# Scores in half strips, a narrower merge, and new orders in a fused attention and expert kernel

## The chip, the cores and the metric

The kernel runs on one core of a Trainium2 chip. The metric is the device time of one execution in microseconds; the median of three runs stands for a kernel. The engines are PE (TensorE: matmuls and transposes; PEld is its weight load), DVE (VectorE), ACT (ScalarE), POOL (GpSimd) and SP, which only issues transfers. Each works through a queue of its own in order.

## What is computed

Windowed causal attention with a linear bias per head, then a layer of experts in which every token goes to one expert (batch 8, 8 heads, 576 positions of 64; 4608 tokens of 512, 8 experts of 1024):

```python
scores = scale * np.matmul(q, k.transpose(0, 1, 3, 2))
bias = slopes[:, None, None] * (-np.abs(rel))[None, :, :]
mask = (rel >= 0) & (rel < 128)              # rel = query position - key position
attn = softmax(np.where(mask, scores + bias, -1e9))
x = (attn @ v) as rows of 512
expert_idx = argmax(normalized x @ normalized expert_emb.T / tau)
out = gate * (relu(x @ w1[e]) @ w2[e])       # e: the row's expert
```

## The kernel before

Attention goes over 36 tiles of 128 queries: per batch four whole ones (the first of them is of kind `first`, the others `full`), and for each two batches one of kind `pair`, whose halves are the last 64 queries of each batch. A tile has two halves of four heads, so there are 72 units `u`. A unit's steps, each a job with an engine:

- `score` (PE, `score_pe`, L544): queries times keys into two PSUM banks (`j` = 0, 1), one for each row half of PE. A `full` tile takes, for each of two head pairs `l`, 128 queries by 256 keys (this tile's and the one before); a `pair` tile takes 64 queries by 192 keys for each of the two batches.
- `merge` (DVE, `merge_dve`, L558 and L561): a window of 128 keys ends up in 128 columns, key position modulo 128. Columns whose key lies after the query are overwritten with those 128 keys earlier, under an integer mask. A `full` tile merges 128 columns of two heads in one instruction, a `pair` tile 64.
- `max` (DVE, L568) adds the bias table and takes the maximum; `exp` (ACT, L577); `flip` (PE, L585) transposes four strips of 128 by 128; `phi` (ACT, L488) and `plo` (DVE, L491) split the result into two f16 parts; `mask` (POOL, L617 to L635) separates this tile's keys from the earlier ones.
- `av` (PE, `values_pe`): a first matmul with `erow` (3 rows, L652) puts a small constant into the column of sums, then the weights are multiplied with v's two parts (L667), whose last column holds ones. `recip` and `norm` (DVE, L691, L697) divide.
- For every tile: `v_one` (POOL, L499) writes v's ones column, `v_hi` (ACT, or DVE for a share of the late tiles, L505 and L507) and `v_lo` (POOL, L513) split v; `xhi` (ACT, L710), `xlo` (POOL, L723), `xnorm` (ACT, L719), `xdma` (SP, L727) and `logit` (PE, L735) prepare the routing.

Tiles are routed in groups of 8, 8, 8, 6, 4 and 2; `put` (POOL, L833 and L834) writes a tiny memset to `spare` and then scatters a tile's rows to the experts' areas in DRAM. After the third group the expert with most rows so far is known; its weights are fetched and split (`wlo`: DVE, L877, 16 of them), and PE multiplies its first 384 rows between the last units (`head_hidden` L906, `head_output` L930). Then the experts follow, one after the other (L1329, L1373), which the change leaves alone.

The order is written out before anything runs. `Plan.run` takes the jobs with their planned durations, and on each engine, among the jobs that could start within `SLACK` of the earliest, picks the one with the smallest due time. A due time is `STEP * u + 1000 * DUE[stage]`. The jobs' instructions are then emitted in that order, and each engine's queue keeps it. `SHARE` says which share of the tiles has a step on the other engine, from tile `LATE` on under the names that end in 2.

The bias tables and the mask come from `bias_rel` (POOL) and `bias_table` (DVE): for `full` at the start, for `pair` as jobs `rel_pair` and `tab_pair` a little later; `first_table` is the `full` one with everything ahead of the tile's own keys struck out (POOL, L288).

Of the kernel before, what the change touches and what calls it, by code (L numbers as in the profile page):

```python
# [13 lines left out]
F16 = mybir.dt.float16  # L14
# [39 lines left out]
STEP = 2397  # L54
SLACK = {'PE': 105, 'ACT': 108, 'DVE': 21, 'POOL': 541, 'SP': 10}
# [5 lines left out]
DUE = {'load': -7.6, 'loadv': -4.4, 'k': -19.8, 'q': -19.8, 'v': 3.3, 'score': -16.9, 'merge': 1.9, 'max': 2.6, 'exp': 0.3, 'flip': 15.7, 'phi': -8.7, 'plo': 6.8, 'mask': 6.8, 'av': -22.6, 'norm': 10.7, 'xhi': 9.3, 'xlo': 16.5, 'xnorm': 21.0, 'xdma': 10.9, 'logit': -15.3, 'route': -3.1, 'put': 20.0, 'place': 18.0, 'gap': 4.3}  # L61
# [8 lines left out]
SHARE = {'v': 0, 'x': 0, 'v2': 0.33, 'x2': 0, 'p': 0, 'p2': 0.33}  # L70


class Plan:
# [19 lines left out]
    def run(self, free):  # L93
# [58 lines left out]
        self.order = order  # L152
        for _, n in order:
            jobs[n]["emit"]()
        return free, end
# [3 lines left out]
def kernel(  # L159
# [69 lines left out]
    nc.gpsimd.memset(erow, eparts[2])  # L229
    for n in (1, 0):  # L230
# [36 lines left out]
    def bias_rel(kind):  # L267
        rels[kind] = rel = const.tile([P, P], F32, tag="rel", name=f"rel_{kind}")
        for r0, r1 in ((0, P),) if kind == "full" else ((0, REM), (REM, P)):
            nc.gpsimd.iota(  # L270
                rel[r0:r1, :], pattern=[[-1, P]], base=0, channel_multiplier=1, allow_small_or_imprecise_dtypes=True
            )

    def bias_table(kind):
        rel = rels[kind]
        m = const.tile([P, P], I32, name=f"mask_{kind}")
        wrap = const.tile([P, P], F32, tag="wrap", name=f"wrap_{kind}")
        nc.vector.tensor_scalar(m, rel, 0.0, None, op0=ALU.is_ge)
        nc.vector.tensor_scalar(wrap, rel, 0.0, float(WIN), op0=ALU.is_lt, op1=ALU.mult)
        nc.vector.tensor_tensor(wrap, wrap, rel, op=ALU.add)  # L280
        tab = const.tile([P, H, P], BF16, name=f"tab_{kind}")
        for h in range(H):
            nc.vector.tensor_scalar(tab[:, h, :], wrap, -slopes[h] / QS, None, op0=ALU.mult)
        mk[kind], tabs[kind] = m, tab

    def first_table():
        tab = const.tile([P, H, P], BF16, name="tab_first")
        nc.gpsimd.affine_select(  # L288
            tab, tabs["full"], pattern=[[0, H], [-1, P]], compare_op=ALU.is_ge, fill=NEG, base=0, channel_multiplier=1
        )  # L290
        tabs["first"] = tab
# [86 lines left out]
    def attention(actx):  # L378
# [61 lines left out]
        bias_rel("full")  # L440
        bias_table("full")
# [43 lines left out]
        vS = {}  # L485

# [6 lines left out]
        def v_tag(T):  # L493
            return "vl" if tiles[T][2] == NF - 1 else "v"

        def v_one(T):
            tg = v_tag(T)
            hi = vp.tile([P, H, D + 1], F16, tag=tg + "h", name=f"vh_{T}", bufs=VBUFS[tg])
            nc.gpsimd.memset(hi[:, :, D : D + 1], 1.0 / SX)  # L499
            vS[T] = [hi, None]  # L500

        def v_hi(T):
            dst = vS[T][0][:, :, 0:D]
# [23 lines left out]
        def score_pe(T, hf):  # L527
            kind, b, t = tiles[T]
            R = P // REM
            if kind == "pair":  # L530
                spans = [
                    (slice(i * REM, (i + 1) * REM), slice(0, P + REM), b + i, slice(R * (t - 1), R * t + 1)) for i in range(2)
                ]
            else:
                a = t if kind == "first" else t - 1
                spans = [(slice(0, P), slice(0, (t + 1 - a) * P), b, slice(R * a, R * (t + 1)))]
            for j in range(2):
                sc[T, hf, j] = bank("sc", [P, 2, 2 * P], name=f"sc{j}_{T}_{hf}")
            for l in range(2):
                hp = 2 * hf + l  # L540
                for o, w, x, kc in spans:
                    for j in range(2):
                        rows = slice(64 * j, 64 * j + 64)
                        nc.tensor.matmul(  # L544
                            sc[T, hf, j][o, l, w].rearrange("p (n c) -> p n c", c=REM),
                            qT[T][rows, hp, o],
                            kT[x][rows, kc, hp, :],
                            start=True,
                            stop=True,
                            skip_group_check=True,  # L550
                        )

        def merge_dve(T, hf, j):
            kind, b, t = tiles[T]
            ps = sc[T, hf, j]
            if kind == "full":
                m = mk["full"].unsqueeze(1).to_broadcast([P, 2, P])
                nc.vector.copy_predicated(ps[:, :, 0:P], m, ps[:, :, P : 2 * P])  # L558
            elif kind == "pair":
                m = mk["pair"][:, 0:REM].unsqueeze(1).to_broadcast([P, 2, REM])  # L560
                nc.vector.copy_predicated(ps[:, :, 0:REM], m, ps[:, :, P : P + REM])  # L561

        def max_dve(T, hf, j, l):
            if (T, hf) not in nm_t:
                nm_t[T, hf] = sm.tile([P, 2, 2], F32, tag="nm", name=f"nm_{T}_{hf}", bufs=4)
            if (T, hf) not in sb_t:
                sb_t[T, hf] = pp.tile([P, 2, 2, P], F32, tag="sb", name=f"sb_{T}_{hf}", bufs=SBUFS)
            nc.vector.tensor_tensor_reduce(  # L568
                sb_t[T, hf][:, j, l, :], sc[T, hf, j][:, l, 0:P], tabs[tiles[T][0]][:, 4 * hf + 2 * l + j, :], -QS, BIG, ALU.add, ALU.min, nm_t[T, hf][:, j, l : l + 1]
            )  # L570

        def exp_act(T, hf, j):
            ps, nm = sb_t[T, hf][:, j], nm_t[T, hf][:, j, :]
            if (T, hf) not in pr_t:
                pr_t[T, hf] = pp.tile([P, 4, P], F32, tag="pe", name=f"pe_{T}_{hf}", bufs=3)
            for l in range(2):
                nc.scalar.activation(  # L577
                    pr_t[T, hf][:, 2 * l + j, :], ps[:, l, 0:P], AF.Exp, bias=nm[:, l : l + 1], scale=-1.0
                )

        def probs_pe(T, hf):
            pe = pr_t.pop((T, hf))
            pt = bank("ptp", [P, 4, P], name=f"ptp_{T}_{hf}")
            for i in range(4):
# [157 lines left out]
        def route_ops(gi):  # L742
# [232 lines left out]
        J("rel_pair", "POOL", 600, lambda: bias_rel("pair"), due=STEP * 4, early=EXPERT)  # L975
        J("tab_pair", "DVE", 1500, lambda: bias_table("pair"), after=["rel_pair"], due=STEP * 6)
# [6 lines left out]
        for T in range(NT):  # L983
# [3 lines left out]
            if T >= 2:  # L987
# [8 lines left out]
            J(f"v_one{T}", "POOL", 45, lambda T=T: v_one(T), makes=[(vt + "h", ("vh", T))], due=due("v", u0) - 1000)  # L996
            dv = share(T, SHARE["v" if T < LATE else "v2"])
            J(
                f"v_hi{T}", "DVE" if dv else "ACT", 335 if dv else 520, lambda T=T: v_hi(T),
                after=[f"load_v{T}", f"v_one{T}"], uses=[("ldv", T), ("vh", T)], due=due("v", u0),  # L1000
# [5 lines left out]
            for hf in range(2):  # L1006
# [3 lines left out]
                dep = [f"load_q{T}"] + [f"load_k{x}" for x in k_tiles(T)] + (["tab_pair"] if pair else [])  # L1010
# [7 lines left out]
                for j in range(2):  # L1018
                    c, key, n = a + (j,), keys[j], f"{u}_{j}"
                    J(  # L1020
                        f"merge{n}", "DVE", 0 if first else 202 if pair else 335, lambda c=c: merge_dve(*c),
# [24 lines left out]
                if rest:  # L1046
# [11 lines left out]
                    f"av{u}", "PE", 540 if first else 1130 if pair else 870, lambda a=a: values_pe(*a),  # L1058
# [55 lines left out]
        for gi, G in enumerate(groups):  # L1114
# [44 lines left out]
        for i in range(NP):  # L1159
# [4 lines left out]
            J(f"wlo{i}", "DVE", 850, lambda i=i: part_lo(i), after=[f"whi{i}"], uses=[("stg", i)], due=d + 5500, fill=True)  # L1164
# [476 lines left out]
```

## Time and profile before

| | us |
|---|---|
| median of 3 runs (lowest, highest) | 640.35 (640.18, 642.5) |
| the profiled execution, its own time | 641.88 |
| its span, first to last instruction | 640.2 |
| busy: PE, DVE, ACT, POOL | 595.4, 365.3, 323.0, 256.1 |
| mean granted clock of PE | 0.969 of 2.4 GHz |

The page divides the span into 40 slices of 16 us and shows each engine's busy share in tenths. Attention takes up the first seventeen. Matmuls are pipelined, so a group of matmuls that overlap counts once as busy, and what PE takes for a step is better read from the starts: from one step's first start to the next step's.

### The profile page before, as it was taken

How to read it: one execution, taken by the hardware profiler on the slowest of the kernel's cores; microseconds unless marked ns; L12 is line 12 of the kernel's file. 1: busy time of each engine (PE TensorE's matmuls, PEld its weight loads, DVE VectorE, ACT ScalarE, POOL GpSimd, SP SyncE). 2: the span in 40 equal slices, each digit the busy share in tenths (PEclk: the TensorE clock that was granted, in tenths of full speed). 3: DMA queues.
4: the chain of work that ended last, by engine and by line, in shares of the span. 5: the costliest groups of instructions: out<-in, count | busy, mean ns of one | idle time of the engine just before them, and what ended most of it. 6: DMA issues, size and time to landing. Idle time of an engine off the chain costs nothing. (4 is left out here: it accounts for less than half of the span.)

```text
span 640.2 us, 15149 instructions
## 1 busy us (share of the span) xinstructions
PE 595.4 (93%) x5633; PEld 387.8 (61%) x5633; DVE 365.3 (57%) x1320; ACT 323.0 (50%) x741; POOL 256.1 (40%) x454
## 2 busy tenths in 40 slices
PE   7799999899888879899899999999999999999993
PEld 3677777677665556365554764764856845744442
DVE  5989999889898787323465243451543383310250
ACT  5799899989897754032543242431432362201200
POOL 5769799989896585401102100202102022011011
PEclk9999999989997879999999999999999999999997
DMA  8688977989999643699999449339369091001000
GB/s 253 153 240 188 244 190 213 226 234 205 242 228 253 135 147 67 191 228 261 276 316 254 193 69 288 123 68 282 131 152 324 2 287 51 1 33 46 1 34 33
DMA packets 121291, 109.79 MB, mean 172 GB/s; under 512 B 85109, under 2 KB 86133, under 8 KB 121216
## 3 DMA queue, kind: packets, MB, share of 16 engines
q1 hardware_dynamic: 115376, 89.89, 55.7%
q0 software_dynamic: 5840, 18.92, 8.0%
q8 instruction: 45, 0.74, 0.5%
q14 instruction: 30, 0.25, 0.1%
HBM read 61.92 MB, written 28.12 MB: 141 GB/s over the span
## 5 line engine op out<-in xcount | busy, mean ns | idle before, releaser
L1329 PE MATMUL ps<-xT,w1h 128*128 128x272 f16 (+7 forms) x896 | 174.8, 295 | 3.9 <-DVE hl L1337 2.3
L1329 PE MATMUL ps<-xT,w1l 128*128 128x272 f16 (+7 forms) x448 | 132.3, 295 | 0.0
L371 POOL DMA_INDIRECT out_dram<-y,ids x32 | 34.5, 1078 | 204.6 <-DVE y L1387 103.8
L1329 PEld LDWEIGHTS <-w1h 128*128 128x128 f16 x896 | 87.9, 98 | 35.1 <-issue 2.5
L1337 DVE SCALAR_TENSOR_TENSOR hl<-ps,hh 128x272 f16<-128x272 f32 (+7 forms) x112 | 51.7, 475 | 96.0 <-ACT hh L1339 96.0
L577 ACT ACTIVATE pe<-sb,nm 128x128 f32<-128x128 f32 x288 | 94.5, 391 | 13.5 <-DVE nm L568 12.8
L1373 PE MATMUL ps<-w2h,hl 128*128 128x512 f16 (+1 forms) x264 | 98.5, 373 | 0.8 <-DVE hl L1337 0.7
L1373 PE MATMUL ps<-w2h,hh 128*128 128x512 f16 (+1 forms) x264 | 98.5, 373 | 0.1
L1373 PE MATMUL ps<-w2l,hh 128*128 128x512 f16 (+1 forms) x264 | 98.5, 373 | 0.0
L1339 ACT ACTIVATE hh<-ps 128x272 f16<-128x272 f32 (+7 forms) x112 | 45.7, 424 | 103.9 <-PE ps L1329 103.9
L1373 PEld LDWEIGHTS <-hh 128*128 128x128 f16 x528 | 51.4, 98 | 58.7 <-issue 0.8
L544 PE MATMUL sc<-k,q 64*128 64x256 f32 (+2 forms) x640 | 76.0, 379 | 0.0
L488 ACT ACTIVATE pq<-ptp 128x512 f16<-128x512 f32 x78 | 57.1, 736 | 11.9 <-PE ptp L585 9.5
L585 PE MATMUL ptp<-ident,pe 128*128 128x128 f32 x288 | 52.6, 297 | 5.5 <-ACT pe L577 5.0
L1304 DVE SCALAR_TENSOR_TENSOR w1l<-ws,w1h 128x1024 f16<-128x1024 f32 x28 | 33.4, 1222 | 40.1 <-ACT w1h L1306 40.0
L544 PEld LDWEIGHTS sc<-k,q 64*128 64x128 f32 (+1 forms) x640 | 47.6, 182 | 13.2 <-issue 6.1
L667 PE MATMUL av<-vh,mp 128*128 128x65 f16 x512 | 50.6, 198 | 4.4 <-POOL mp L617 1.7
L1304 DVE SCALAR_TENSOR_TENSOR w2l<-ws,w2h 128x1024 f16<-128x1024 f32 x28 | 33.8, 1223 | 34.3 <-ACT w2h L1306 33.9
L1329 PEld LDWEIGHTS <-w1l 128*128 128x128 f16 x448 | 44.0, 98 | 15.2 <-DVE w1l L1304 0.4
L1306 ACT ACTIVATE w1h<-ws 128x1024 f16<-128x1024 f32 x28 | 28.4, 1052 | 47.2 <-DMA ws<-moe_w_dram 47.1
L491 DVE SCALAR_TENSOR_TENSOR pq<-ptp,pq 128x512 f16<-128x512 f32 x66 | 48.8, 742 | 5.7 <-ACT pq L488 5.6
L1306 ACT ACTIVATE w2h<-ws 128x1024 f16<-128x1024 f32 x28 | 29.1, 1054 | 39.6 <-DMA ws<-moe_w_dram 37.5
(214 smaller groups left out, 1084.9 us busy)
## 6 DMA issues: line engine op xcount, KB each, us to landing
ws<-moe_w_dram SPq DMA_DIRECT2D x56, 512.0 KB, 10.5
q<-q_dram SPq DMA_DIRECT2D x36, 256.0 KB, 3.3
ldv<-v_dram SPq DMA_DIRECT2D x36, 256.0 KB, 4.0
k<-k_dram SPq DMA_DIRECT2D x32, 256.0 KB, 4.0
stg<-moe_w_dram SPq DMA_DIRECT2D x16, 256.0 KB, 4.4
xs<-zrow SPq DMA_DIRECT2D x3, 1092.2 KB
xs<-zrow SPq DMA_DIRECT2D x1, 1413.5 KB
xs<-zrow SPq DMA_DIRECT2D x1, 1285.0 KB
```

What stands on the lines that cost most here:

```text
L488: nc.scalar.activation(hi, ps, AF.Copy, scale=scale)
L491: nc.vector.scalar_tensor_tensor(lo, ps, scale, hi, op0=ALU.mult, op1=ALU.subtract)
L544: nc.tensor.matmul(sc[T, hf, j][o, l, w].rearrange("p (n c) -> p n c", c=REM), qT[T][rows, hp, o], kT[x][rows, kc, hp, :], start=True, sto ...
L577: nc.scalar.activation(pr_t[T, hf][:, 2 * l + j, :], ps[:, l, 0:P], AF.Exp, bias=nm[:, l : l + 1], scale=-1.0)
L585: nc.tensor.matmul(pt[:, i, :], pe[:, i, :], ident, start=(i == 0), stop=(i == 3), is_transpose=True, skip_group_check=True)
L667: nc.tensor.matmul(o_, a_, b_, start=False, stop=(n == last), skip_group_check=True)
L1304: nc.vector.scalar_tensor_tensor(lo_, x, SW, hi, op0=ALU.mult, op1=ALU.subtract)
L1306: nc.scalar.activation(hi, x, AF.Copy, scale=SW)
L1329: nc.tensor.matmul(ps[:, :w], a[:, kt, fs], xx[:, b + kt, c0 : c0 + w], start=(n == 0), stop=(n == len(jobs) - 1))
L1337: nc.vector.scalar_tensor_tensor(hl[:, ft, c0 : c0 + w], ps[:, :w], 0.0, hi, op0=ALU.max, op1=ALU.subtract)
L1339: nc.scalar.activation(hi, ps[:, :w], AF.Relu)
L1373: nc.tensor.matmul(ps, x[:, ft, a * P : (a + 1) * P], w[:, ft, c], start=(n == 0), stop=(n == len(jobs) - 1))
```

## The change

- Scores: every tile now works in half strips. For each half `i` of the queries, 64 queries by 192 keys of two heads `l`, which lie one above the other in the partitions; four matmuls (row half `j`, `l`) for each `i`. Strips are numbered 2j + i, and `flip` puts them back into the order of heads.
- Merge: in a `full` tile only 64 columns of each half can hold later keys; both halves are merged in one instruction of 2 x 64 columns.
- The tables get a further dimension, a slope column per partition in place of a constant, and serve all three kinds: the `pair` table and its jobs go.
- v's buffers are two tiles with slots; their ones are written once, ahead of the loop, and `v_one` goes.
- `erow` and `eone` get 128 rows, of which 125 are zero.
- `put` leaves the memset to `spare` out unless the job before it on POOL was a `put` too.
- Planned durations, `STEP`, `SLACK`, `DUE` and `SHARE` are new, and with them the order.

```diff
-STEP = 2397
-SLACK = {'PE': 105, 'ACT': 108, 'DVE': 21, 'POOL': 541, 'SP': 10}
+STEP = 2500
+SLACK = {'PE': 151, 'ACT': 51, 'DVE': 18, 'POOL': 693, 'SP': 147}
-DUE = {'load': -7.6, 'loadv': -4.4, 'k': -19.8, 'q': -19.8, 'v': 3.3, 'score': -16.9, 'merge': 1.9, 'max': 2.6, 'exp': 0.3, 'flip': 15.7, 'phi': -8.7, 'plo': 6.8, 'mask': 6.8, 'av': -22.6, 'norm': 10.7, 'xhi': 9.3, 'xlo': 16.5, 'xnorm': 21.0, 'xdma': 10.9, 'logit': -15.3, 'route': -3.1, 'put': 20.0, 'place': 18.0, 'gap': 4.3}
+DUE = {'load': -4.9, 'loadv': -2.2, 'k': -19.1, 'q': -15.7, 'v': 3.8, 'score': -28.6, 'merge': 2.1, 'max': 2.7, 'exp': -3.4, 'flip': 3.7, 'phi': -5.2, 'plo': 6.2, 'mask': 7.6, 'av': -18.6, 'norm': 10.9, 'xhi': 10.1, 'xlo': 17.0, 'xnorm': 24.5, 'xdma': 5.7, 'logit': -15.3, 'route': -0.6, 'put': 18.7, 'place': 17.6, 'gap': 6.4}
-SHARE = {'v': 0, 'x': 0, 'v2': 0.33, 'x2': 0, 'p': 0, 'p2': 0.33}
+SHARE = {'v': 0, 'x': 0, 'v2': 0, 'x2': 0.33, 'p': 0, 'p2': 0.33}
...
-    erow = const.tile([3, P], BF16, name="erow")
-    eone = const.tile([3, 4], BF16, name="eone")
+    erow = const.tile([P, P], BF16, name="erow")
+    eone = const.tile([P, 4], BF16, name="eone")
...
+        for hf in range(2):
+            for l in range(2):
+                for j in range(2):
+                    nc.vector.memset(slope[l * REM : (l + 1) * REM, hf, j : j + 1], -slopes[4 * hf + 2 * l + j] / QS)
...
+        tab = const.tile([P, 2, 2, 2, P], BF16, name="tab_full")
+        for hf in range(2):
+            for j in range(2):
+                nc.vector.tensor_scalar(tab[:, hf, j], wrap, slope[:, hf, j : j + 1], None, op0=ALU.mult)
...
+        for hf in range(2):
+            for r0 in (0, REM):
+                nc.gpsimd.affine_select(
+                    tab[r0 : r0 + REM, hf], tabs["full"][r0 : r0 + REM, hf], pattern=[[0, 2], [REM, 2], [-1, P]], compare_op=ALU.is_ge,
...
+        v_all = {tg: [vp.tile([P, n, H, D + 1], F16, tag=tg + "h", name=f"{tg}h", bufs=1), 0] for tg, n in VBUFS.items()}
+        for x, _ in v_all.values():
+            nc.gpsimd.memset(x[:, :, :, D : D + 1], 1.0 / SX)
...
-            for l in range(2):
-                hp = 2 * hf + l
-                for o, w, x, kc in spans:
-                    for j in range(2):
+            for i in range(2):
+                x, n0, n1 = (b + i, R * (t - 1), R * t + 1) if kind == "pair" else (b, max(R * (t - 1) + i, 0), R * t + i + 1)
...
+                for j in range(2):
+                    for l in range(2):
                         rows = slice(64 * j, 64 * j + 64)
...
                         nc.tensor.matmul(
-                            sc[T, hf, j][o, l, w].rearrange("p (n c) -> p n c", c=REM),
-                            qT[T][rows, hp, o],
-                            kT[x][rows, kc, hp, :],
+                            sc[T, hf, j][l * REM : (l + 1) * REM, i, c0 : c0 + (n1 - n0) * REM].rearrange("p (n c) -> p n c", c=REM),
+                            qT[T][rows, hp, i * REM : (i + 1) * REM],
+                            kT[x][rows, n0:n1, hp, :],
...
             if kind == "full":
-                m = mk["full"].unsqueeze(1).to_broadcast([P, 2, P])
-                nc.vector.copy_predicated(ps[:, :, 0:P], m, ps[:, :, P : 2 * P])
+                nc.vector.copy_predicated(z[:, 0:6:5], mk["full"], z[:, 2:4])
...
                 nc.tensor.matmul(
-                    pt[:, i, :], pe[:, i, :], ident, start=(i == 0), stop=(i == 3), is_transpose=True, skip_group_check=True
+                    pt.rearrange("p (l j) c -> p l j c", j=2)[:, :, j, i * REM : (i + 1) * REM],
+                    pe[:, n, :],
+                    ident.rearrange("p (l c) -> p l c", l=2),
...
-                nc.gpsimd.memset(spare, 0.0)
+                if plan.before.get("POOL", "").startswith("put"):
+                    nc.gpsimd.memset(spare, 0.0)
...
-                f"v_hi{T}", "DVE" if dv else "ACT", 335 if dv else 520, lambda T=T: v_hi(T),
+                f"v_hi{T}", "DVE" if dv else "ACT", 1000 if dv else 520, lambda T=T: v_hi(T),
...
-                    f"score{u}", "PE", 560 if first else 920 if pair else 1130, lambda a=a: score_pe(*a), makes=[(RING["sc"], x) for x in keys],
+                    f"score{u}", "PE", 560 if first else 920, lambda a=a: score_pe(*a), makes=[(RING["sc"], x) for x in keys],
...
-                    f"put{T0 + g}", "POOL", 1270, of(gi, 3, g), dma=750, after=[done, prev[0], f"gate{gi}_0", f"xlo{T0 + g}"], uses=[("gx", T0 + g)],
+                    f"put{T0 + g}", "POOL", 1020 if gi < LAST else 1270, of(gi, 3, g), dma=750, after=[done, prev[0], f"gate{gi}_0", f"xlo{T0 + g}"], uses=[("gx", T0 + g)],
...
-            J(f"wlo{i}", "DVE", 850, lambda i=i: part_lo(i), after=[f"whi{i}"], uses=[("stg", i)], due=d + 5500, fill=True)
+            J(f"wlo{i}", "DVE", 1150, lambda i=i: part_lo(i), after=[f"whi{i}"], uses=[("stg", i)], due=d + 5500, fill=True)
```

## Rows read from the trace of the kernel before

**Rows 1.** The page: busy tenths of PE, 40 slices of 16 us.

```profile
PE   7799999899888879899899999999999999999993
```

**Rows 2.** Stretches: start:end, length, then each engine's busy us, clock, DMA, GB/s.

```profile
20.00:220.00 200.00, 182.07 (x2802) 139.53 (x2803) 182.93 (x937) 181.58 (x482) 166.63 (x272) 0.95 0.89 214
...
80.00:100.00 20.00, 19.30 (x288) 14.82 (x284) 18.88 (x99) 19.45 (x54) 19.25 (x30) 1.00 0.75 199
120.00:140.00 20.00, 18.07 (x251) 13.74 (x249) 16.82 (x93) 16.08 (x44) 16.28 (x29) 0.83 0.97 239
220.00:272.00 52.00, 44.80 (x404) 26.16 (x402) 30.74 (x97) 18.47 (x45) 31.91 (x56) 0.91 0.51 140
```

**Rows 3.** Groups of ACT, 20 to 220 us: busy, mean ns | idle before, releaser.

```profile
L577 ACT ACTIVATE pe<-sb,nm 128x128 f32<-128x128 f32 x260 | 85.5, 391 | 6.9 <-DVE nm L568 6.3
L488 ACT ACTIVATE pq<-ptp 128x512 f16<-128x512 f32 x70 | 51.2, 736 | 7.2 <-PE ptp L585 4.8 <-PE ptp L601 1.7 <-POOL spare L833 0.6
...
L710 ACT ACTIVATE rows_buf<-xf 128x512 f16<-128x512 f32 x33 | 20.4, 618 | 4.1 <-DVE xf L697 4.1
```

**Rows 4.** PE in order of time: scores of three kinds and the instruction behind.

```profile
113.72 1.14 PE L544 MATMUL sc<-k,q 64*128 64x256 f32 x8
114.79 0.17 PE L652 MATMUL av<-eone,erow 3*128 3x4 bf16 x1
...
154.67 0.88 PE L544 MATMUL sc<-k,q 64*64 64x192 f32 x16
155.49 0.17 PE L652 MATMUL av<-eone,erow 3*128 3x4 bf16 x1
...
160.29 0.72 PE L544 MATMUL sc<-k,q 64*128 64x128 f32 x8
160.94 0.17 PE L652 MATMUL av<-eone,erow 3*128 3x4 bf16 x1
```

**Rows 5.** PE in order of time: the constant's row and its neighbours.

```profile
117.08 0.19 PE L667 MATMUL av<-vh,pq 128*128 128x65 f16 x1
117.21 0.17 PE L652 MATMUL av<-eone,erow 3*128 3x4 bf16 x1
117.32 0.21 PE L667 MATMUL av<-vh,pq 128*128 128x65 f16 x1
117.36 0.20 PE L667 MATMUL av<-vo,pq 128*128 128x64 f16 x1
```

**Rows 6.** Groups of DVE, 0 to 275 us, shapes kept apart.

```profile
L558 DVE COPY_PREDICATED sc<-mask_full,sc 128x256 f32<-128x256 int32 x96 | 38.3, 423 | 3.0 <-PE sc L544 3.0
L877 DVE SCALAR_TENSOR_TENSOR w1l<-stg,w1h 128x512 f16<-128x512 f32 x8 | 14.3, 1798 | 0.0
...
L561 DVE COPY_PREDICATED sc<-mask_pair,sc 128x128 f32<-128x128 int32 x16 | 4.4, 292 | 0.2
```

**Rows 7.** DVE in order of time: the pair's tables begin, the next work begins.

```profile
17.31 0.60 DVE L278 TENSOR_SCALAR mask_pair<-rel_pair 128x128 int32<-128x128 f32 x1
...
20.43 0.24 DVE L691 RECIPROCAL rs<-av 128x4 f32<-128x4 f32 x2
```

**Rows 8.** PE in order of time: the wait behind the pair's tables.

```profile
21.33 0.17 PE L652 MATMUL av<-eone,erow 3*128 3x4 bf16 x1 [2.12 <-DVE pq L491]
```

**Rows 9.** DVE in order of time: the first maximum.

```profile
8.04 0.29 DVE L568 CUSTOM_DVE_ANT_0 sb<-sc,tab_first 128x128 f32<-128x128 f32 x1 [3.02 <-PE sc L544]
```

**Rows 10.** Groups of POOL, whole span: the spacers.

```profile
L833 POOL MEMSET spare<- 128x1 f32 x36 | 3.9, 108 | 0.0
```

**Rows 11.** All engines in order of time, 227 to 234 us: one low half.

```profile
227.56 5.39 DVE L877 SCALAR_TENSOR_TENSOR w1l<-stg,w1h 128x512 f16<-128x512 f32 x1
...
231.25 1.14 POOL L723 TENSOR_TENSOR rows_buf<-xf,rows_buf 128x512 f16<-128x512 f32 x1
...
233.34 0.18 PE L652 MATMUL av<-eone,erow 3*128 3x4 bf16 x1 [3.06 <-DVE xf L697]
```

**Rows 12.** A stretch of PE alone: busy us, granted clock, DMA share, GB/s.

```profile
128.00:130.00 2.00, 2.00 (x21) 0.50 1.09 388
```

More of the change, by code (lines that the diff above doesn't have):

```diff
@@ L152, in run @@
         self.order = order
+        self.before = {}
         for _, n in order:
             jobs[n]["emit"]()
+            if jobs[n]["ns"]:
+                self.before[jobs[n]["eng"]] = n
         return free, end
@@ L265, with bias_rel @@
     rels = {}
-    def bias_rel(kind):
-        rels[kind] = rel = const.tile([P, P], F32, tag="rel", name=f"rel_{kind}")
-        for r0, r1 in ((0, P),) if kind == "full" else ((0, REM), (REM, P)):
+    def bias_rel():
+        rels["full"] = rel = const.tile([P, 2, P], F32, tag="rel", name="rel_full")
+        for r0 in (0, REM):
             nc.gpsimd.iota(
-                rel[r0:r1, :], pattern=[[-1, P]], base=0, channel_multiplier=1, allow_small_or_imprecise_dtypes=True
+                rel[r0 : r0 + REM], pattern=[[REM, 2], [-1, P]], base=0, channel_multiplier=1, allow_small_or_imprecise_dtypes=True
@@ L272, in bias_rel, with bias_table @@
             )
[L274 to L278, printed above, removed]
+    def bias_table():
+        rel = rels["full"]
+        m = const.tile([P, 2, REM], I32, name="mask_full")
+        wrap = const.tile([P, 2, P], F32, tag="wrap", name="wrap_full")
+        slope = const.tile([P, 2, 2], F32, name="slope")
+        for hf in range(2):
+            for l in range(2):
+                for j in range(2):
+                    nc.vector.memset(slope[l * REM : (l + 1) * REM, hf, j : j + 1], -slopes[4 * hf + 2 * l + j] / QS)
@@ L279, in bias_table @@
         nc.vector.tensor_scalar(wrap, rel, 0.0, float(WIN), op0=ALU.is_lt, op1=ALU.mult)
         nc.vector.tensor_tensor(wrap, wrap, rel, op=ALU.add)
[L281 to L284, printed above, removed]
-    def first_table():
[L287 to L290, printed above, removed]
+        tab = const.tile([P, 2, 2, 2, P], BF16, name="tab_full")
@@ new lines, in bias_table @@
+        for hf in range(2):
+            for j in range(2):
+                nc.vector.tensor_scalar(tab[:, hf, j], wrap, slope[:, hf, j : j + 1], None, op0=ALU.mult)
+        for i, op in ((0, ALU.is_ge), (1, ALU.is_lt)):
+            nc.vector.tensor_scalar(m[:, i, :], rel[:, i, i * REM : (i + 1) * REM], 0.0, None, op0=op)
+        mk["full"], tabs["full"] = m, tab
+    def first_table():
+        tab = const.tile([P, 2, 2, 2, P], BF16, name="tab_first")
+        for hf in range(2):
+            for r0 in (0, REM):
+                nc.gpsimd.affine_select(
+                    tab[r0 : r0 + REM, hf], tabs["full"][r0 : r0 + REM, hf], pattern=[[0, 2], [REM, 2], [-1, P]], compare_op=ALU.is_ge,
+                    fill=NEG, base=0, channel_multiplier=1,
+                )
@@ L438, in warm @@
                 nc.tensor.matmul(pt, ones, ones.unsqueeze(1).to_broadcast([P, 4, P]), start=True, stop=True)
-        bias_rel("full")
-        bias_table("full")
+        bias_rel()
+        bias_table()
         first_table()
@@ L494, in v_tag @@
             return "vl" if tiles[T][2] == NF - 1 else "v"
[L496 to L500, printed above, removed]
         def v_hi(T):
+            buf = v_all[v_tag(T)]
+            vS[T] = [buf[0][:, buf[1] % VBUFS[v_tag(T)]], None]
+            buf[1] += 1
             dst = vS[T][0][:, :, 0:D]
@@ L583, in probs_pe @@
             pt = bank("ptp", [P, 4, P], name=f"ptp_{T}_{hf}")
-            for i in range(4):
+            for n in range(4):
+                j, i = divmod(n, 2)
                 nc.tensor.matmul(
-                    pt[:, i, :], pe[:, i, :], ident, start=(i == 0), stop=(i == 3), is_transpose=True, skip_group_check=True
+                    pt.rearrange("p (l j) c -> p l j c", j=2)[:, :, j, i * REM : (i + 1) * REM],
+                    pe[:, n, :],
+                    ident.rearrange("p (l c) -> p l c", l=2),
+                    start=(n == 0),
+                    stop=(n == 3),
+                    is_transpose=True,
+                    skip_group_check=True,
                 )
@@ L974, in attention @@
         J("tails", "POOL", 900, lambda: [nc.gpsimd.memset(x, 0.0) for x in tails], due=STEP * 4, early=EXPERT)
-        J("rel_pair", "POOL", 600, lambda: bias_rel("pair"), due=STEP * 4, early=EXPERT)
-        J("tab_pair", "DVE", 1500, lambda: bias_table("pair"), after=["rel_pair"], due=STEP * 6)
         last = None
@@ L995, in attention @@
             vt = v_tag(T)
-            J(f"v_one{T}", "POOL", 45, lambda T=T: v_one(T), makes=[(vt + "h", ("vh", T))], due=due("v", u0) - 1000)
             dv = share(T, SHARE["v" if T < LATE else "v2"])
             J(
-                f"v_hi{T}", "DVE" if dv else "ACT", 335 if dv else 520, lambda T=T: v_hi(T),
-                after=[f"load_v{T}", f"v_one{T}"], uses=[("ldv", T), ("vh", T)], due=due("v", u0),
+                f"v_hi{T}", "DVE" if dv else "ACT", 1000 if dv else 520, lambda T=T: v_hi(T),
+                after=[f"load_v{T}"], makes=[(vt + "h", ("vh", T))], uses=[("ldv", T), ("vh", T)], due=due("v", u0),
             )
@@ L1020, in attention @@
                     J(
-                        f"merge{n}", "DVE", 0 if first else 202 if pair else 335, lambda c=c: merge_dve(*c),
+                        f"merge{n}", "DVE", 0 if first else 202, lambda c=c: merge_dve(*c),
                         after=[f"score{u}"], uses=[key], due=due("merge", u) + 670 * j,
@@ L1057, in attention @@
                 J(
-                    f"av{u}", "PE", 540 if first else 1130 if pair else 870, lambda a=a: values_pe(*a),
+                    f"av{u}", "PE", 470 if first else 1050 if pair else 800, lambda a=a: values_pe(*a),
                     after=[f"mask{u}", ] + then("put", T - XBUFS) + [f"v_lo{x}" for x in k_tiles(T)], makes=[(RING["av"], ("av", u))],
```

39 lines of the change are left out of this document (20 added, 19 removed).

## The prediction

> **What bounds the kernel now.** I read the forty slices of the page first. PE stands at 7 to 9 tenths through the first seventeen slices (attention, to about 272 us) and at 9 in all but the last of the rest [rows 1]. That second part, the experts, is matmul after matmul, and the change doesn't touch a line of it. So its length is fixed, and what the change can do is to let it begin earlier. The question is what sets the length of attention.
>
> Next came the busy time of each engine in stretches. From 20 to 220 us PE is busy 182.1 us, DVE 182.9, ACT 181.6 and POOL 166.6 [rows 2]. Three engines are full to nine tenths at once. No wait bounds this stage: four static queues of nearly the same length do, and each waits now and then for another. An engine made lighter gives back time only until the next one is full. How full an engine can get is seen in the same view: 80 to 100 has ACT at 19.45 of 20, 120 to 140 only at 16.08 [rows 2]. Last, ACT's groups with the idle time before them: of its 18.4 idle us, 6.3 wait for the maximum of DVE, 4.8 and 1.7 for PE's transposes, 4.1 for DVE's normalized rows [rows 3].
>
> **The change part by part.**
>
> *Scores.* A full tile's half takes 8 matmul records of 256 columns; the next PE instruction starts 1.07 us after the first (113.72 to 114.79). The last tile of a pair of batches already does what the change makes general: 16 records, 64x64 with 192 columns, four side by side, and there the step is 0.82 (154.67 to 155.49) [rows 4]. Saved: 0.25 us for each of 8 x 3 x 2 = 48 halves, 12.0 us of PE. The 16 halves of first tiles take 0.65 now (160.29 to 160.94) [rows 4] and become 16 records of 128 columns: 0 to 0.17 more each (0.82 with 192 columns is the ceiling), 0 to 2.7 us; I take 0.5, as the columns that stream stay the same. Sum 11.5 us of PE, between 9 and 12.
>
> The Trainium skill (TensorEngine Tiling (Array Packing), Instruction Overhead) speaks against this: each matmul costs about 60 cycles whatever its width. By that rule eight more records would cost about 0.2 us (an estimate from the page's 60 cycles at 2.4 GHz), and the saving would be 0.05 us a half, 2.4 us in all. The row of the pair's tile, with the same 16 records, disagrees, and I go by the row.
>
> *Constant's row.* The matmul that starts each average has 3 rows. From the matmul before it to it are 0.13 us, from it to the next 0.11, where the others of the line follow at 0.03 to 0.04 [rows 5]. With 128 rows like its neighbours it should cost one such step: 0.07 saved where a score (64 rows anyway) stands before it, 0.17 elsewhere. Over 72 halves 5 to 12 us; below it, zero if the gap is not due to the 3 rows. I take 7.
>
> *Merge.* 96 merges of 256 elements hold DVE for 38.3 us; 16 of 128 elements take 4.4, 0.275 each [rows 6]. At that price 96 cost 26.4: saved 11.9 us of DVE. The maxima, exponentials and transposes keep their sizes; only which head and which queries share a strip changes: nothing.
>
> *Tables.* The pair's mask and table hold DVE from 17.31 to 20.43, 3.1 us [rows 7], and behind them in its queue stands the part that PE waits for 2.12 us [rows 8]. They go. In their place the first table gets 8 tiny memsets, 4 wider multiplications and four selects on POOL; all stand before the first maximum, ahead of which DVE idles 3.02 us for the score [rows 9]. I put their cost at 0 behind that cover, up to 1 us where it is gone.
>
> *POOL.* 36 memsets of v's ones go, two wider ones come before the loop; of 36 spacers, 3.9 us [rows 10], those go that don't follow another scatter. With the ones taken to be like the spacers, 4 to 6 us of POOL, off the path on average (166.6 of 200 [rows 2]). The new v buffer is one tile in slots; the rows' buffer is built so too, and the instruction that writes it waits for DVE's result only [rows 3], so I price a false wait at 0. Three copies of v move from DVE to ACT and three of x the other way, same shape: 0.
>
> *On the path.* PE loses 18.5 us of some 225, DVE 15, POOL 5, ACT nothing. So ACT becomes the fullest, and what can be won between 20 and 220 is its idle time, 18.4 us, not the 18.5 of PE.
> - Start (18 to 22 us): with the pair's table gone PE's wait goes; 2.0, between 0 and 3.
> - Steady part: 16.4 us of ACT's idle time are left. If ACT got as dense as in 80 to 100, 200 us would become 181.6/0.9725 = 186.7; less the 2.0 above, 11.3. The other end is 1: the same waits come back on another engine. I take 5.5, a third of the idle time, since the waits for DVE and PE shrink but don't vanish.
> - Tail (220 to 272): PE is busy 44.8 of 52 at a clock of 0.91 [rows 2]. A few late scores and averages get shorter: 1.5, with an end at either side of 5, because the new order decides here.
>
> Sum 9.0. The orders themselves (new due times, later scatters, a higher step) can't be priced from this trace; the two stretches of rows 2, one order on like work, differ by 3.4 us of ACT in 20, so I give them plus or minus 5. Against the profiled execution (641.88, span 640.2): 632.9. The median of the runs is 640.35, 1.5 lower: 631.4, rounded to 631.5.
>
> **The rivals.**
> - *Slower: DVE held up by POOL.* The low halves of the first expert's weights (16 on DVE) have two operands in SBUF. One took 5.39 us from 227.56, where the 8 of its kind average 1.8 [rows 6]; it ended half a microsecond after POOL's last of a run of work, and PE then idled 3.06 us [rows 11]. After gaps in its work PE runs at half clock: in 128 to 130 the granted clock is 0.50, its 1.2 GHz level [rows 12]. Price: 3 us idle and some 3 us of lost work, about 6.5. The Trainium skill (SBUF — State Buffer, Who interferes with whom) has it that an instruction of DVE with two SBUF inputs blocks against one of POOL that reads SBUF; the trace agrees. The change leaves these 16 in and reshuffles what POOL does beside them. It decides from 1.4 further events of this sort (9.0/6.5); with two, 640.35 - 9.0 + 13 = 644.4. Against it: POOL gets lighter by 5 us, so its runs have more holes. Chance 0.12.
> - *Near the same.* A freed PE idles instead: ACT and the scatters keep the pace, gaps lengthen, and the clock falls more often, giving back what the start and the scores won. Gain 2, 638.4. For: PE's clock stands at 0.95 from 20 to 220 though PE is busy for nine tenths of it [rows 2]. Chance 0.18.
> - *Scores that don't run four abreast.* In the new strips the four quadrants read different heads, in the pair's tile two different batches; if they queued up, PE would save 7 and DVE stays as forecast: gain 4, 636.4. Against it: the pair's tile, which runs so [rows 4]. Chance 0.05.
> - *More.* Both ends of the table at once: ACT dense, a tail without a long DVE stall: gain 9 to 19, around 624. Chance 0.13.
>
> **How the numbers follow.** Forecast 0.52: 627 to 637, likeliest 631.5. The range takes in the dense case's better part and the near-same case: 622 to 641.5. A measurement of this kernel tells about 0.5% from no change, 3.2 us: faster means below 637.15. Forecast, more, and the scores' rival lie there (0.52 + 0.13 + 0.05 = 0.70), near the same 0.18, slower 0.12.
>
> **What would show it.** Right: scores' step 0.82 in full tiles, 0.03 to 0.04 around the constant's row, merges near 0.28 us; from 20 us on ACT the busiest engine with PE well below it; the experts' first matmul near 263 us instead of 272; the part from there as long as before. Wrong: ACT no denser than now with new waits on POOL or DMA in its groups; more slices of PEclk below 9 before 270 us; a weight's low half of 4 us or more; or an unchanged first expert matmul, which would mean that the tail's chain, not attention's pace, sets it.

## The result and the profile after

The changed kernel takes 631.37 us (median of 4 runs, 629.72 to 633.12), the kernel before 640.28 beside it. The ratio is 0.9853, with a 95% interval from 0.9819 to 0.9887: 9.4 us faster, between 7.2 and 11.6. The forecast was 631.5. The size is right; whether the reasons are is what the experiments ask.

Where the 10.3 us between the two profiled executions arise is read from the starts of work that both kernels do: the reciprocals on DVE (72, one a half of a tile), the first expert's first matmul, the experts' first matmul, and the end.

| work | before | after | gain so far |
|---|---|---|---|
| 9th reciprocal | 38.98 | 36.25 | 2.7 |
| 36th | 116.74 | 112.21 | 4.5 |
| 54th | 171.76 | 165.30 | 6.5 |
| 63rd | 200.10 | 192.05 | 8.1 |
| first expert's first matmul | 219.48 | 210.67 | 8.8 |
| experts' first matmul | 272.18 | 263.79 | 8.4 |
| end of the span | 640.2 | 629.8 | 10.3 |

The page of after, its line of PE, against [rows 1]:

```profile
PE   7999898799887778899999999999999999999993
```

Stretches of after, in the columns of [rows 2]. The fourth line ends where the first expert's matmuls begin:

```profile
20.00:220.00 200.00, 172.29 (x3296) 128.89 (x3293) 173.39 (x932) 184.72 (x494) 171.83 (x235) 0.97 0.91 222
80.00:100.00 20.00, 19.32 (x380) 14.18 (x377) 18.42 (x102) 20.00 (x56) 18.15 (x23) 1.00 0.79 177
120.00:140.00 20.00, 17.50 (x357) 13.25 (x356) 17.73 (x106) 18.77 (x52) 18.72 (x24) 1.00 0.91 242
20.00:211.00 191.00, 163.29 (x3233) 123.20 (x3230) 169.06 (x918) 179.73 (x482) 164.40 (x222) 0.99 0.93 223
220.00:272.00 52.00, 43.51 (x408) 26.90 (x407) 29.96 (x85) 14.05 (x34) 24.88 (x44) 0.93 0.53 137
```

Before, PE, DVE and ACT were about equally busy (182 of 200). Now, up to the first expert's first matmul, ACT stands at 179.73 of 191 (94%), DVE at 89%, POOL at 86% and PE at 85%. ACT idles 11.3 us there, where 18.4 of 200 were idle before. In its groups (20 to 220 us, against [rows 3]) the waits for DVE went from 6.3 to 2.6 and from 4.1 to 0.8. The wait for PE's transposes reads 7.1 where it was 4.8, but 4.77 of it is one wait behind the first expert's start (the last line below); up to 211 us it is 2.3. So in the steady part all three shrank:

```profile
L590 ACT ACTIVATE pe<-sb,nm 128x128 f32<-128x128 f32 x268 | 88.9, 408 | 2.8 <-DVE nm L582 2.6
L504 ACT ACTIVATE pq<-ptp 128x512 f16<-128x512 f32 x73 | 54.3, 752 | 7.6 <-PE ptp L599 7.1 <-PE ptp L621 0.5
...
L730 ACT ACTIVATE rows_buf<-xf 128x512 f16<-128x512 f32 x30 | 19.1, 637 | 0.9 <-DVE xf L717 0.8
...
214.34 0.74 ACT L504 ACTIVATE pq<-ptp 128x512 f16<-128x512 f32 x1 [4.77 <-PE ptp L599]
```

PE of after in order of time, against [rows 4, 5]: a full tile's scores and what follows, the constant's row between two averages, a first tile's scores:

```profile
105.54 0.88 PE L555 MATMUL sc<-k,q 64*64 64x192 f32 x16
106.35 0.18 PE L672 MATMUL av<-eone,erow 128*128 128x4 bf16 x1
106.39 0.19 PE L687 MATMUL av<-vh,tails 128*128 128x65 f16 x1
...
61.88 0.19 PE L687 MATMUL av<-vh,pq 128*128 128x65 f16 x1
61.90 0.17 PE L672 MATMUL av<-eone,erow 128*128 128x4 bf16 x1
61.93 0.19 PE L687 MATMUL av<-vh,pq 128*128 128x65 f16 x1
...
130.04 0.67 PE L555 MATMUL sc<-k,q 64*64 64x128 f32 x16
130.64 0.66 PE L599 MATMUL ptp<-ident,pe 128*128 128x128 f32 x4
```

A full half steps on after 0.81 us (1.07 before), a first half after 0.60 (0.65), and the constant's row costs 0.02 to 0.04 at either side (0.11 to 0.13). DVE's groups (0 to 275 us, against [rows 6]):

```profile
L569 DVE COPY_PREDICATED sc<-mask_full,sc 128x128 f32<-128x128 int32 x96 | 24.5, 287 | 1.6 <-PE sc L555 1.5
L898 DVE SCALAR_TENSOR_TENSOR w1l<-stg,w1h 128x512 f16<-128x512 f32 x8 | 16.4, 2048 | 0.0
```

The merges fell from 38.3 to 24.5 us. The low halves of the first expert's weights got dearer (16.4 us for 14.3), and the long one is still there. The tail of after, in order of time, against [rows 11]:

```profile
219.40 6.00 DVE L898 SCALAR_TENSOR_TENSOR w1l<-stg,w1h 128x512 f16<-128x512 f32 x1
...
224.77 0.91 POOL L650 TENSOR_SCALAR_AFFINE_SELECT tails<-pq 64x256 f32<-64x256 f32 x1
...
226.97 0.19 PE L672 MATMUL av<-eone,erow 128*128 128x4 bf16 x1 [3.35 <-DVE xf L717]
```

So the stall of the tail was neither won nor doubled: 6.00 us for 5.39, and PE idles 3.35 for 3.06.

### The profile page after: what moved, and what is told of

It is laid out like the page before. It is cut to its first block, busy times and chain, and to the rows that moved or that the text cites. A ratio compares the mean times of both kernels' runs of the same rounds, so it can differ in the third digit from the quotient of the medians.

```text
span 629.8 us, 16133 instructions
## 1 busy us (share of the span) xinstructions
PE 576.4 (92%) x6145; PEld 372.7 (59%) x6145; DVE 354.2 (56%) x1314; ACT 321.5 (51%) x741; POOL 254.8 (40%) x399
## 5 line engine op out<-in xcount | busy, mean ns | idle before, releaser
L555 PE MATMUL sc<-k,q 64*64 64x192 f32 (+1 forms) x1152 | 61.4, 329 | 0.0
L599 PE MATMUL ptp<-ident,pe 128*128 128x128 f32 x288 | 54.6, 295 | 4.9 <-ACT pe L590 2.8
L582 DVE CUSTOM_DVE_ANT_0 sb<-sc,tab_full 128x128 f32<-128x128 f32 x224 | 55.0, 277 | 0.0
L687 PE MATMUL av<-vh,mp 128*128 128x65 f16 x384 | 39.7, 197 | 5.8 <-POOL mp L637 5.5
```

Source lines behind the costliest of these rows:

```text
L555: nc.tensor.matmul(sc[T, hf, j][l * REM : (l + 1) * REM, i, c0 : c0 + (n1 - n0) * REM].rearrange("p (n c) -> p n c", c=REM), qT[T][rows, h ...
L582: nc.vector.tensor_tensor_reduce(sb_t[T, hf][:, 2 * j + i, :], sc[T, hf, j][:, i, c0 : c0 + P], tab, -QS, BIG, ALU.add, ALU.min, nm_t[T, h ...
L599: nc.tensor.matmul(pt.rearrange("p (l j) c -> p l j c", j=2)[:, :, j, i * REM : (i + 1) * REM], pe[:, n, :], ident.rearrange("p (l c) -> p ...
```

## The experiments

Each ratio is to the kernel before, run on the same chip; "on the changed kernel" is the difference to 0.9853 times 640.3 us. The intervals are some 0.3 to 0.6% to either side, 2 to 4 us, and the 0.9853 has its own of 0.34%.

**Orders.** First the changed operations under the planner's old numbers: the step and with it SLACK, DUE, SHARE and the planned durations of before.

```diff
-STEP = 2500
+STEP = 2397
...
```

> The changed kernel with the due times, slacks, step, shares and planned durations of before; all its operations stay new. Theory (less work on PE and DVE makes the gain, the orders little): 632 to 635, most of the 9 us is kept. Rival (the new orders make the gain): 638 to 641.

Measured 631.12 us, 0.9841 [0.9802, 0.9880]: -0.8 us on the changed kernel, just below the theory's range.

Then the reverse: the kernel before with the new step, SLACK, DUE and SHARE, and the new planned durations of `v_hi` and `wlo` on DVE.

```diff
-STEP = 2397
+STEP = 2500
...
```

> The kernel before with the step, slacks, due times and shares of the changed one, and its planned durations for the two DVE copies; all operations old. Theory (the orders alone bring little): 638 to 643. Rival (the orders make the gain): 631 to 635.

Measured 645.04, 1.0059 [1.0030, 1.0089]: 3.8 us slower than before, outside both ranges. The new numbers alone bring nothing; the gain is in the operations.

**Parts.** In the changed kernel the constant's row alone undone:

```diff
-erow = const.tile([P, P], ...); eone = const.tile([P, 4], ...)
+erow = const.tile([3, P], ...); eone = const.tile([3, 4], ...)
```

> The changed kernel, only the constant's matmul back at 3 rows, same order. Theory: the gaps of 0.13 and 0.11 us around it come back, 5 to 7 us of PE, but PE is no longer the fullest engine: 1 to 3 us slower than the change, 632.5 to 634.5. Rival (PE still sets the pace): 5 to 7 us slower, 636.5 to 638.5.

Measured 632.43, 0.9864 [0.9822, 0.9905]: +0.7, under the 1 to 3 expected. The wide row saves some 5 us of PE (0.07 behind most of the 72 rows; few have an average ahead of them), and they are hardly seen at the end.

The strips, the narrow merge and the shared table alone; the three-row constant, v's ones for each tile, a spacer (the tiny memset) ahead of every scatter and the planner's numbers are those of before, but for the scores' and merges' planned durations:

```diff
-erow = const.tile([P, P], ...)
+erow = const.tile([3, P], ...)
...
+J(f"v_one{T}", "POOL", 45, ...)
...
-if plan.before.get("POOL", "").startswith("put"):
-    nc.gpsimd.memset(spare, 0.0)
+nc.gpsimd.memset(spare, 0.0)
```

> The strips, the narrow merge and the shared table alone: the constant with 3 rows, v's ones per tile, all spacers, due times, shares and planned durations as before, save those of score and merge. Theory: PE saves about 11.5 us and DVE 15, so 634 to 637. Rival (the small parts and the orders make the gain): 638 to 641.

Measured 637.18, 0.9926 [0.9895, 0.9957]: 4.7 us faster than before, half of the gain. The order of this run is the planner's own, neither that of before nor that of after. As the constant gives 0.7 and the orders nothing, some 4 us were left to POOL's parts, which the forecast had put at nothing. So those were undone in the changed kernel:

```diff
+J(f"v_one{T}", "POOL", 45, lambda T=T: v_one(T), ...)
...
-if plan.before.get("POOL", "").startswith("put"):
-    nc.gpsimd.memset(spare, 0.0)
+nc.gpsimd.memset(spare, 0.0)
```

> The changed kernel with its POOL parts undone: a spacer ahead of every scatter again, and v's ones written once a tile again (about 5 us of POOL, and with them the older ring of v buffers). Theory A, that POOL's work beside DVE has a price (13 us of it cost about 4 us): +1 to +4 us on the changed kernel, ratio to the kernel before 0.987 to 0.992. That would also explain most of what the strips alone lacked. Rival B, the prediction's own view, that POOL's parts lie off the path: 0 to +1 us, ratio 0.985 to 0.987; what the strips alone lacked would then be the order that other planned durations give. Rival C, the spacers hold scatters apart and help: below 0.984.

Measured 645.30, 1.0058 [1.0024, 1.0092]: +13.1, outside all three. Attention isn't what became slower: the 63rd reciprocal starts at 195.00 (192.05 in the changed kernel) and the 72nd at 235.58 (235.79). The order did it, as the next run will confirm. With one job more a tile for POOL, planned at 45 ns, the planner puts the transposing load of the first expert's rows behind fetches of weights on the DMA queue. That queue in the changed kernel, and PE's first use:

```profile
203.73 3.26 SPq L906 DMA_TRANSPOSE x_head<-xs  x1
...
211.79 14.07 SPq L891 DMA_DIRECT2D stg<-moe_w_dram  x3
...
210.67 0.80 PE L927 MATMUL ps_head<-x_head,w1h 128*128 128x384 f16 x2 [3.89 <-DMA x_head<-xs]
```

and with POOL's parts back:

```profile
218.06 4.62 SPq L890 DMA_DIRECT2D stg<-moe_w_dram  x3
...
225.94 0.34 SPq L890 DMA_DIRECT2D stg<-moe_w_dram  x1
229.22 3.15 SPq L905 DMA_TRANSPOSE x_head<-xs  x1
...
235.36 0.83 PE L926 MATMUL ps_head<-x_head,w1h 128*128 128x384 f16 x2
```

What the DMA queue waited for in this run, 215 to 232 us (the third number is the longest wait):

```profile
SPq L890 <- DVE w1l L897: 18.9, 4, 14.0
SPq L905 <- DMA xs<-rows_buf,di: 2.6, 1, 2.6
```

A fetch ahead of the load stands 14.0 us, until DVE has read the weights that it writes over; then the load itself waits 2.6 us for a scatter of the next group, since 30 scatters were issued ahead of it and not 24 as in the changed kernel. The load is issued 25.5 us later, and the first expert's matmuls, which filled PE's holes between the last averages, come after them: from 217 to 240 PE is busy 16.29 us at a clock of 0.69, in the changed kernel 19.66 at 0.93. The experts start at 270.53 instead of 263.79 and run 372.6 us instead of 366.0. In that second part PE waits 4.9 us for the parts of the hidden layer (2.25 at 284.71, 1.95 at 291.75, 0.72 at 293.07; in the changed kernel 1.53, once), and its granted clock is 0.66 from 285 to 300, where the changed kernel has 1.00 from 278 to 293. Why these waits arise was not followed up. The run says what a place in a queue costs, not what POOL's memsets cost. For that they went back in without the planner:

```diff
 def v_hi(T):
     buf[1] += 1
+    nc.gpsimd.memset(vS[T][0][:, :, D : D + 1], 1.0 / SX)
...
-if plan.before.get("POOL", "").startswith("put"):
-    nc.gpsimd.memset(spare, 0.0)
+nc.gpsimd.memset(spare, 0.0)
```

> The changed kernel with the work of POOL's parts put back but nothing else: a spacer ahead of each of the 36 scatters (24 more than now), and a memset of v's ones for each of the 36 tiles, at the place where that tile's v is written. The order on PE, DVE, ACT and the DMA queue is the changed kernel's, step for step, unlike in the run where the same parts were put back through the planner and the first expert's rows came 25 us later. Theory A, that this run lost its 13 us by the order of the tail and not by POOL's work: +1 to +4 us on the changed kernel (5 us of POOL at the price of the load test, 4 us for 13, or somewhat more), ratio to the kernel before 0.987 to 0.992. Rival B, the prediction's view that POOL's parts lie off the path: 0 to +1 us, ratio 0.984 to 0.987. Rival C, that the memsets themselves hold something up (a tile's v waits for them, scatters are held apart): +8 us or more, ratio 0.998 or more.

Measured 638.71, 0.9919 [0.9884, 0.9954]: +4.2, at the upper edge of theory A. Groups of POOL in this run, whole span:

```profile
L854 POOL MEMSET spare<- 128x1 f32 x36 | 4.1, 114 | 0.0
L516 POOL MEMSET vh<- 128x8 f16 x28 | 3.8, 139 | 0.0
...
L516 POOL MEMSET vlh<- 128x8 f16 x8 | 1.1, 138 | 0.0
```

24 spacers of 0.114 and 36 memsets of 0.138 are 7.7 us of POOL, and they cost 4.2. How they cost it isn't shown. That masks come later behind the memsets, and PE with them, would be the obvious way, but PE's waits for masks are no longer in this run: together 8.8 us from 20 to 200, 11.6 in the changed kernel. The largest of these groups, in the changed kernel and in this run:

```profile
L687 PE MATMUL av<-vh,mp 128*128 128x65 f16 x346 | 35.4, 196 | 5.5 <-POOL mp L637 5.2
...
L688 PE MATMUL av<-vh,mp 128*128 128x65 f16 x331 | 34.9, 198 | 3.7 <-POOL mp L638 3.2 <-POOL spare L854 0.2
```

What grew in this trace is ACT's wait for PE's transposes (2.3 to 3.9 us) and the time at a lower clock (0.96 granted from 20 to 211, 0.99 in the changed kernel); no run parts the two.

Strips 4.7, POOL's parts 4.2 and the constant 0.7 make 9.6, beside 9.4 measured for the whole; with 2 to 4 us on each that is agreement, not proof that nothing overlaps.

**Loads.** Four runs repeat work of one engine in the changed kernel, order untouched, to see which still sets the pace; each repeat writes what stood there. On PE four score matmuls of a full half, 128 columns each; on DVE one merge of two; on ACT every second tile's sum of squares; on POOL, in two tiles of three, half of x's low part.

```diff
+nc.tensor.matmul(sc[T, hf, j][...], qT[T][...], kT[x][...], ...)
...
+for _ in range(2 - j): nc.vector.copy_predicated(z[:, 0:6:5], ...)
...
+for _ in range(1 + (T % 2)): nc.scalar.activation(junk, xf_t[T], AF.Square, ...)
...
+nc.gpsimd.tensor_tensor(xx[:, DM : DM + DM // 2], ..., op=ALU.subtract)
```

> The changed kernel with four of a full tile's sixteen score matmuls repeated on 128 columns (about 0.25 us each of 48 halves, 12 us of PE, what the strips had saved), same order. Theory (PE has slack now): 1 to 4 us slower than the change, 632.5 to 635.5. Rival (no queue is the limit): 6 us slower, 637.

> The changed kernel with one of the two merges of every full half repeated (48 more of 0.26 us, 12 us of DVE, what the narrow merge had saved), same order. Theory (DVE has slack now): 1 to 4 us slower than the change, 632.5 to 635.5. Rival (no queue is the limit): 6 us slower, 637.

> The changed kernel with the squares of every second tile computed twice on ACT (18 more instructions of 0.62 us and their read, about 12 us of ACT), same order. Theory (ACT is the fullest queue): 8 to 12 us slower than the change, 639 to 643. Rival (no queue is the limit, each unit of extra work costs about half wherever it is put): 6 us slower, 637.

> The changed kernel with half of the low part of x computed twice on POOL in two of three tiles (24 more instructions of some 0.55 us, about 13 us of POOL), same order. Theory (POOL has slack): 1 to 4 us slower than the change, 632.5 to 635.5. Rival (no queue is the limit): 6 us slower, 637.

The loads as the traces show them, PE's by the steps of one half, DVE's and POOL's by their groups:

```profile
114.14 0.88 PE L555 MATMUL sc<-k,q 64*64 64x192 f32 x16
114.84 0.40 PE L567 MATMUL sc<-k,q 64*64 64x128 f32 x8
...
115.17 0.46 PE L767 MATMUL board<-enc,xT 128*128 128x8 f16 x12
```

```profile
L570 DVE COPY_PREDICATED sc<-mask_full,sc 128x128 f32<-128x128 int32 x144 | 38.9, 292 | 3.3 <-PE sc L555 1.7
```

```profile
L745 POOL TENSOR_TENSOR rows_buf<-xf,rows_buf 128x256 f16<-128x256 f32 x24 | 17.3, 720 | 1.9
```

| load on | its size, us | ratio | on the changed kernel |
|---|---|---|---|
| PE | 48 x (1.03 - 0.81) = 10.6 | 0.9847 [0.9795, 0.9900] | -0.4 |
| DVE | 38.9 - 24.5 = 14.4 | 0.9975 [0.9941, 1.0010] | +7.8 |
| ACT | 18 x (0.62 + 0.19) = 14.6 | 0.9951 [0.9915, 0.9987] | +6.3 |
| POOL | 17.3 | 0.9914 [0.9879, 0.9948] | +3.9 |

PE has no price now that these runs can see; the interval leaves up to 3 us, 0.3 for a microsecond. DVE, which theory had at 1 to 4, costs as much for a microsecond as ACT, about half of one, and ACT less than the 8 to 12 that theory gave it: on these two the rival's view holds, that no queue alone is the limit. POOL costs a quarter, and less than the memsets did, 4.2 for 7.7. What a heavier merge does is seen at ACT: its exponentials wait for DVE's maxima again, 20 to 200 us, first in the changed kernel, then with the load on DVE:

```profile
L590 ACT ACTIVATE pe<-sb,nm 128x128 f32<-128x128 f32 x252 | 83.7, 409 | 2.8 <-DVE nm L582 2.6
```

```profile
L591 ACT ACTIVATE pe<-sb,nm 128x128 f32<-128x128 f32 x244 | 80.3, 394 | 8.3 <-DVE nm L583 7.7
```

Was PE already free before the change? The same on the kernel before, with the last pair of score matmuls of each full half:

```diff
+for j in range(2):
+    nc.tensor.matmul(sc[T, hf, j][o, l, w]..., qT[T][...], kT[x][...], ...)
```

> The kernel before, in its own order, with two of the eight score matmuls of each full half done twice (48 x 2 records of 256 columns, about 13 us of PE by the step of 0.134 us for one; the repeat writes what stood there). Theory A, that PE had slack already in the kernel before, so that nothing of what the change takes from PE reaches the end: ratio 1.00 to 1.005. Rival B, the prediction's view, that PE was one of three engines that bound equally there: +5 to +10 us, ratio 1.008 to 1.016; then PE's saving was worth something, and the changed kernel stopped being sensitive to PE only after it.

Measured 649.00, 1.0135 [1.0072, 1.0198]: 8.6 us slower than before. A half of that run:

```profile
114.77 1.13 PE L544 MATMUL sc<-k,q 64*128 64x256 f32 x8
115.74 0.60 PE L555 MATMUL sc<-k,q 64*128 64x256 f32 x4
116.27 0.46 PE L746 MATMUL board<-enc,xT 128*128 128x8 f16 x12
```

Its stretch from 20 to 200 us:

```profile
20.00:200.00 180.00, 169.81 (x2646) 134.31 (x2648) 158.52 (x807) 159.77 (x422) 150.56 (x246) 1.00 0.88 210
```

The repeat is four records and not two, so the load was larger than planned: a step of 1.50 instead of 1.07, 20.6 us in all. PE fills up to 169.81 of 180 and the others fall back. A microsecond of PE cost 0.42 there (0.22 to 0.62 by the interval), and nothing measurable after the change.

**A try at the tail.** DVE's stall taken away in the changed kernel: DVE only scales the fetched weights, POOL subtracts.

```diff
-nc.vector.scalar_tensor_tensor(lo, hd["x", i], SW, hi, op0=ALU.mult, op1=ALU.subtract)
+nc.vector.tensor_scalar(hd["x", i], hd["x", i], SW, None, op0=ALU.mult)
+nc.gpsimd.tensor_tensor(lo, hd["x", i], hi, op=ALU.subtract)
```

> The changed kernel with the low halves of the first expert's 16 weight parts split up: DVE only scales the fetched part in place (one operand in SBUF and a number), ACT casts, and POOL subtracts. DVE loses 24 us of instructions with two SBUF operands, one of which took 6.0 us and left PE 3.35 us idle, and gets 16 short ones, 5 to 8 us; POOL gets 16 x 1.2 = 19 us, of which some 10 before the last scores. Theory A, that DVE held up by POOL costs the tail its 3 to 6 us and DVE's time counts more than POOL's: 3 to 8 us faster than the changed kernel, ratio 0.973 to 0.981. Rival B, that POOL's queue, with masks and scatters behind the subtractions, gives it back: ratio 0.984 to 0.995.

Measured 653.56, 1.0152 [1.0096, 1.0207]: 19.1 us slower than the changed kernel. The DMA queue and POOL of that run:

```profile
198.93 23.37 SPq L747 DMA_TRANSPOSE xT<-rows_buf  x3
227.79 3.21 SPq L909 DMA_TRANSPOSE x_head<-xs  x1
...
232.12 1.15 POOL L898 TENSOR_TENSOR w1l<-stg,w1h 128x512 f16<-128x512 f32 x1
```

In the plan the subtractions are work to fill holes with, and POOL does the first of them at 232.12. The expert's rows are again issued behind 30 scatters, at 227.79, and its first matmul starts at 244.59. This is nearest to rival B, but far outside its range: as in the run with POOL's parts back, a late load goes with a late tail. The long wait on DVE is gone, and it is not what decides. No version here beats the changed kernel; its operations under the old plan equal it.

## Why the prediction was right, and where not

- *Scores, constant, merge, tables.* These were sized about right. A full half saves 0.26 us of PE (0.25 forecast), and first halves take 0.05 less where 0.03 more was forecast. The row of 128 costs 0.02 to 0.04 at either side; that saves some 5 us, the low end of the forecast's 5 to 12, since a row seldom has an average ahead of it. A merge holds DVE for 24.5/96 = 0.255 us where 0.275 was forecast, and PE's wait of 2.12 is gone. The step of 0.81 stands against the Trainium skill (TensorEngine Tiling (Array Packing), Instruction Overhead), by whose 60 cycles for each matmul a half would have gained 0.05 (an estimate from that figure).
- *ACT becomes the fullest, PE falls out.* This is half right. PE had a price before (0.42 a microsecond) and has none that can be measured now; the intervals, 0.22 to 0.62 and up to 0.28, just overlap, so the fall is likely and not certain. ACT is the fullest. But the limit isn't ACT alone: DVE costs as much. That the pace is set by the chain from scores over maxima and exponentials to masks, and not by the idle time of one engine, fits these prices; no run shows it directly.
- *By place.* Start 2.7 (2.0 forecast); steady part up to the 63rd reciprocal 5.4 (5.5); from there to the experts 0.3 (1.5); the experts' part, forecast unchanged, 1.9. The match of the steady part is luck of this order, as the same starts in other runs show:

| run | 9th reciprocal | 63rd | experts | end |
|---|---|---|---|---|
| before | 38.98 | 200.10 | 272.18 | 640.2 |
| after | 36.25 | 192.05 | 263.79 | 629.8 |
| changed operations, old plan | 36.59 | 196.97 | 263.65 | 629.7 |
| strips, merge and table alone | 36.76 | 201.21 | 270.74 | 636.8 |

Under the old plan the changed operations gain 0.7 in the steady part and 5.4 from there to the experts, and end where after ends. With the strips, the merge and the table alone the steady part is 3.3 us longer than before, though all its scores and merges are the short ones (the granted clock is 0.94 there, 0.97 before). What they gain lies at the start and behind the 63rd reciprocal. Each of these is one trace.
- *The experts' part.* It lasts 368.0 us before and 366.0 after. PE's waits there, before and after:

```profile
288.43 0.39 PE L1373 MATMUL ps<-w2h,hl 128*128 128x512 f16 x1 [0.72 <-DVE hl L1337]
317.93 0.72 PE L1329 MATMUL ps<-xT,w1h 128*128 128x336 f16 x2 [2.33 <-DVE hl L1337]
...
309.12 0.45 PE L1347 MATMUL ps<-xT,w1h 128*128 128x336 f16 x2 [1.53 <-DVE hl L1355]
```

These are 1.5 of the 1.9 us. No edit touches that part. Yet it lasts 368.0 to 368.8 in all three traces with the old operations (before, before with the new plan, before with the load on PE) and 365.6 to 366.2 in all nine with the new ones, but for the two whose load for the first expert came late (372.6 and 368.7). So the gain goes with the operations, and since the strips, the merge and the table alone have 366.1 too, with one of these; by what way is open. The forecast had nothing for it. The total is right because this gain and the larger start make up for the tail.
- *POOL off the path.* This is the step that failed. Priced at 0, these parts bring 4.2 of the 9.4. Their size was low too, 7.7 us for 4 to 6. From an average over 200 us (POOL at 83%) the forecast took it that nothing waits for them. The forecast came out because the third of ACT's idle time, a guess between two ends, took this in without naming it.
- *Orders, plus or minus 5.* The whole set of numbers made -0.8 and +3.8 us, but 13 us came where a plan lets one load come 25 us later. The bound was too narrow for a changed plan.
- *Slower, DVE held by POOL.* There is one low half above 4 us before and one after, so the sign "a low half of 4 us or more" could not tell the kernels apart. The Trainium skill (SBUF — State Buffer, Who interferes with whom) agrees with the row of 6.00 us beside a run of POOL without a hole, though this one ended before that run did; a second event, from which on the rival would have decided, didn't come. *Near the same:* up to the first expert PE is granted 0.99 from 20 us on, not less than before; the fall of the clock that this rival needed is absent. *Not four abreast:* refuted by 0.81.

## What to carry to other kernels

A load test on each engine, at the same order, tells which saving will count before and after a change; a mean of busy time doesn't: POOL and PE stood at 86 and 85%, and an added microsecond cost 0.2 to 0.5 us on the one and nothing measurable on the other. Where a planner makes the order, compare edits with the order held fixed: 36 jobs planned at 45 ns moved one load by 25 us and turned 9 us of gain into a loss of 4. In a tail, look first at the one transfer that lets the next stage begin: its place in its queue, and what was issued ahead of it that it waits for. And where a forecast by place agrees, repeat the reading under another order: here the same total came with quite another split.

## What was not expected of the hardware

- Extra matmuls went with a higher granted clock: over the whole span 0.984 with the load on PE (mean of 5 runs) against 0.977 for the kernel before (15 runs), and 0.986 against 0.979 in the changed kernel (4 and 4 runs). The changed kernel under the old plan, with no matmul added, has 0.984 too (6 runs), so the order alone can do as much. Part of a load on PE may pay for itself so, and part of a saving be given back; no run parts the two.
- Memsets of eight or one element a partition hold POOL for 0.138 and 0.114 us; 60 of them came to 7.7 us, and to 4.2 us of the kernel's time.
- In the profiled execution of after ACT's instructions are some 2% longer than in most other runs (the squares 631 ns on average, against 619 to 622, and 626 in the run with POOL's parts back), so ACT's 94% is 1 to 2 points too high; why this one execution differs is open.
